# Accumulating DMAs for the cross-block spectrum sums, in-place complex sums, and a two-phase order of exponentials

## The chip, the cores and the metric

The kernel runs on one core of a Trainium2 chip. The metric is the device time in microseconds (us) of one execution; smaller is better. One execution is also recorded by the hardware profiler, and all stretches below are in microseconds from the start of that execution. A kernel's time is the median of its runs. Kernels are compared only within the same rounds.

## The reference, cut to what matters

The program blends two branches with a gate. Branch A is a state-space convolution: a kernel K of length 2048 for each of 512 channels is generated from 128 complex modes, and the input is convolved with it by a Fourier transform. Branch B routes the two highest-scoring rows through a small gated network and adds the result to them.

```python
P  = exp(dt * (A_re + 1j*A_im) * l)                  # modes x 2048 lags
K  = einsum("dn,dnl,dn->dl", C, P, dt*B).real        # kernel of the convolution
y  = irfft(rfft(pad(u)) * rfft(pad(K)))[:L] + u*Dskip
...
return g * y + (1 - g) * b       # g: sigmoid gate; b: x plus the routed rows
```

The kernel does the convolution in two blocks of 1024 rows. The output spectrum of block 1 is a sum over blocks: X1 times K0 plus X0 times K1, both complex. That sum (the "cross-block" sum) is what the change is about. Everything is done in two halves of 256 channels (half 0, half 1), and each half's spectrum in two quarters.

## The kernel before

The program lists operations with their reads, writes and a cost estimate, and a list scheduler fixes the order of instructions on each engine when the kernel is built. The hardware then follows that order. VectorE's `tensor_tensor` operations all come from one helper, `TT`, so in the profile they share one line (L399 before, L400 after).

The products of one quarter, as VectorE does them:

```python
for blk in blks:                       # block 1 first, then block 0
    TT(v4(PA), xv(blk), kv(0, 0), MUL, ...)          # 2048 columns
    if blk == 1:                       # the cross-block sum
        TT(v4(PC), xv(0), kv(1, 0), MUL, ...)
        TT(PA, PA, PC, ADD, ...)                     # 2048 columns
    TT(v4(PBb), xv(blk), kv(0, 1), MUL, ...)
    if blk == 1:
        TT(v4(PC), xv(0), kv(1, 1), MUL, ...)
        TT(PBb, PBb, PC, ADD, ...)
    TT(v1(YY, 0), v1(PA, 0), v1(PBb, 1), SUB, ...)   # complex sums, 1024 columns
    TT(v1(YY, 1), v1(PA, 1), v1(PBb, 0), ADD, ...)
    TT(sd(0), y(0), y(1), ADD, ...)                  # into X, for the inverse
    TT(sd(1), y(0), y(1), SUB, ...)
```

The inverse transform multiplies X by a constant matrix G on TensorE, block 1 before block 0. ScalarE scales half 0's result into a buffer YA, and a DMA that adds (an accumulating DMA, issued by GpSimd) puts it on the output rows:

```python
AC(YA(...), pb(...), ACTF.Copy, ..., scale=gate)
P.op(POOL, lambda g: g.dma_start(u, YA(...), accum_op=ADD), ..., cost=1.0, nbytes=262144, dma=True)
```

The front (the first part of the program, up to the end of the kernel generation) makes two tables. Table 1 and table 2 both need exponentials and sines on ScalarE; the two functions live in different activation tables. All exponentials come first, in phase 0, and then everything of phase 1:

```python
exps1(0); exps2(0)
... routing()                          # tanh, silu in phase 1
tab1(0, (1, 1)); forward(); tab2(0, (1, 1)); tab1(1, (1, 1))
```

Of the kernel before, what the change touches and what calls it, by code (L numbers as in the profile page):

```python
# [13 lines left out]
ACTF = mybir.ActivationFunctionType  # L14
ALU = mybir.AluOpType
# [39 lines left out]
class Op:  # L55
    __slots__ = ("eng", "fn", "deps", "cost", "tset", "prio", "idx", "pos", "start", "end", "sem", "n", "bl", "vc", "tag", "nbytes", "dma", "name", "alt")


class Prog:
# [4 lines left out]
    def __init__(self):  # L64
        self.bufs, self.ops, self.boost, self.bias = [], [], 0.0, {DVE: 0.4}

    def op(self, eng, fn, rd=(), wr=(), cost=0.2, tset=None, prio=0.0, tag="", n=1, nbytes=0, dma=False):
        o = Op()
        o.alt = None
        if isinstance(eng, tuple):  # L70
            o.alt = dict(zip(eng, zip(fn, cost)))
            eng, fn, cost = eng[0], fn[0], min(cost)
# [34 lines left out]
    def schedule(self):  # L107
# [25 lines left out]
        while left:  # L133
            best = None
            for e0 in ENGS:
                for o in ready[e0]:
                    if o.tset is not None and o.tset != phases[ph[0]]:
                        continue
                    e = e0
                    if o.alt is not None:  # L140
                        e = min(o.alt, key=lambda x: max(free[x], rt[o.idx]) + o.alt[x][1] + self.bias.get(x, 0.0))
                    st = max(free[e], rt[o.idx])
                    key = (st, -o.bl - o.prio)
                    if best is None or key < best[0]:
                        best = (key, o, e)
# [190 lines left out]
KB = 1024  # L336


def bass_gated_mix__ssm_conv_s4__moe_arch_mod__prompt_kernel(nc, A_u, A_A_re, A_A_im, A_B_re, A_B_im, A_C_re, A_C_im, A_log_dt, A_Dskip,
# [24 lines left out]
    with ExitStack() as es:  # L364
# [3 lines left out]
        sems = {e: es.enter_context(nc.semaphore("s_" + e)) for e in ENGS}  # L368
        dsem = [es.enter_context(nc.semaphore("d%d" % i)) for i in range(90)]
        block = es.enter_context(nc.Block())  # L370
# [49 lines left out]
        def DMA(pairs, rd, wr, nbytes, eng=SP, **k):  # L420
            return P.op(eng, lambda h: [h.dma_start(o, i) for o, i in pairs], rd, wr, cost=0.5 * len(pairs), n=len(pairs), nbytes=nbytes, dma=True, **k)

        o_ = [190 * KB]
        def small(name, nbytes, dt):
# [35 lines left out]
        KA = [B("ka0", oG, 64 * 84 * 2), B("ka1", oE, 64 * 84 * 2)]  # L460
        KC = [B("kc0", oD + 28 * KB, 3 * KB), B("kc1", oE + 11 * KB, 3 * KB)]
        KP = B("kp", oD, 2 * NKP + 1536)
        CO = [B("co%d" % i, oD + 22 * KB + 512 * i, 512) for i in range(2)]
        KK = [B("kk0", oC, 16 * KB), B("kk1", oF, 16 * KB)]
        G = B("g", oF + 16 * KB, 16 * KB)
        PA = B("pa", oI, 4 * KB); PBb = B("pb", oI + 4 * KB, 4 * KB); PC = B("pc", oI + 8 * KB, 4 * KB); YY = B("yy", oI + 12 * KB, 4 * KB); YA = B("ya", oI + 16 * KB, 4 * KB)

# [159 lines left out]
        def routing():  # L627
# [13 lines left out]
            CP(SG(0, 128, 0, (1, 16)), SGB(0, 128, 16, (1, 16)), [(SGB, "r")], [(SG, "r")])  # L641
            AC(SG(0, 128, 16, (1, 16)), SGB(0, 128, 0, (1, 16)), ACTF.Tanh, [(SGB, "s")], [(SG, "t")], scale=0.5, tset=1)
            TS(SGB(0, 128, 32, (1, 16)), SG(0, 128, 16, (1, 16)), 0.5, MUL, [(SG, "t")], [(SGB, "g")], s2=0.5, op1=ADD)
# [24 lines left out]
            STT(MSB(0, 128, 0, (1, 1)), R(35), CF(0, 128, 145, (1, 1)), R(38), MUL, ADD, [K("m1"), K("s0"), CF], [(MSB, 0)])  # L668
            AC(R(39), MSB(0, 128, 0, (1, 1)), ACTF.Tanh, [(MSB, 0)], [K("th")], scale=0.5, tset=1)
            TS(MSB(0, 128, 1, (1, 1)), R(39), 0.5, MUL, [K("th")], [(MSB, 1)], s2=0.5, op1=ADD)  # L670
# [32 lines left out]
            DMA([(WD(0, 128, 0, (D, 14), (1, D)), dr(B_w_down, 0, (D, 128), (128 * D, 14), (1, D)))], [], [WD], 1835008)  # L703
            AC(hb(2), hb(0), ACTF.Silu, [(HB, 0)], [(HB, 2)], tset=1)
            TT(hb(3), hb(2), hb(1), MUL, [(HB, 2), (HB, 1)], [(HB, 3)])
# [121 lines left out]
        def products(h, qd, blks):  # L827
# [12 lines left out]
            kk = lambda blk, part: [(KK[h], (blk, part, qd))]  # L840
            for blk in blks:
                TT(v4(PA), xv(blk), kv(0, 0), MUL, kx(blk) + kk(0, 0), [PA])
                if blk == 1:
                    TT(v4(PC), xv(0), kv(1, 0), MUL, kx(0) + kk(1, 0), [PC])
                    TT(PA(0, 128, 0, (1, 2048)), PA(0, 128, 0, (1, 2048)), PC(0, 128, 0, (1, 2048)), ADD, [PA, PC], [PA])
                TT(v4(PBb), xv(blk), kv(0, 1), MUL, kx(blk) + kk(0, 1), [PBb])
                if blk == 1:
                    TT(v4(PC), xv(0), kv(1, 1), MUL, kx(0) + kk(1, 1), [PC])
                    TT(PBb(0, 128, 0, (1, 2048)), PBb(0, 128, 0, (1, 2048)), PC(0, 128, 0, (1, 2048)), ADD, [PBb, PC], [PBb])
                TT(v1(YY, 0), v1(PA, 0), v1(PBb, 1), SUB, [PA, PBb], [(YY, 0)])  # L850
                TT(v1(YY, 1), v1(PA, 1), v1(PBb, 0), ADD, [PA, PBb], [(YY, 1)])
                y = lambda pm: YY(0, 128, pm * 512, (1024, 2), (1, 512))
                sd = lambda pm: X(0, 128, h * 8192 + blk * 4096 + pm * 1024 + 2 * qd * 256, (2048, 2), (1, 512))
                kw = lambda pm: [xk(h, blk, part, pm, ft) for part in range(2) for ft in (2 * qd, 2 * qd + 1)]
                TT(sd(0), y(0), y(1), ADD, [YY], kw(0))
                TT(sd(1), y(0), y(1), SUB, [YY], kw(1))
        ivp = [(2, 0), (2, 1), (3, 0), (3, 1)]
        ivb = [PB("iv%d" % i, a, b) for i, (a, b) in enumerate(ivp)]
        ni = [0]
        def inverse(h):  # L860
            for blk in (1, 0):
                bufs = {}
                for q in range(2):
                    for t2 in range(2):
                        for par in range(2):
# [17 lines left out]
                            if h == 0 or blk == 1:  # L883
                                for e in range(2):
                                    tb = blk * 8 + (2 * t2 + e) * 2 + par
                                    AC(YA(0, 128, t2 * 1024 + (2 * e + par) * 256, (1, HC)), pb(0, 128, e * 256, (1, HC)), ACTF.Copy, [pb.buf, (SG, "g")], [(YA, (par, t2, e))], scale=SG(0, 128, 32 + tb, (1, 1)))
                                if par == 1:
                                    tbs = [blk * 8 + 4 * t2 + k for k in range(4)]
                                    u = U(0, 128, (blk * 8 + 4 * t2) * D + h * HC, (D, 4), (1, HC))
                                    P.op(POOL, lambda g, u=u, t2=t2: g.dma_start(u, YA(0, 128, t2 * 1024, (HC, 4), (1, HC)), accum_op=ADD), [(YA, (p_, t2, e)) for p_ in range(2) for e in range(2)] + [(U, ("x", tb)) for tb in tbs], [(U, ("o", tb, h)) for tb in tbs], cost=1.0, nbytes=262144, dma=True)  # L890
                                continue
# [18 lines left out]
        exps1(0)  # L910
        exps2(0)
        DMA([(bass.AP(park.tensor, 0, [[NM * 256, 128], [1, NM * 256]]), ST(0, 128, 0, (1, NM * 256)))], [ST], [PK], 655360)
# [6 lines left out]
        P.boost = 30.0  # L919
        tab2(0, (1, 1))  # L920
        P.boost = -30.0
        tab1(1, (1, 1))
        P.boost = 0.0
# [6 lines left out]
        for h_ in range(2):  # L930
            P.op(POOL, lambda h, h_=h_: h.memset(CO[h_](0, 128, 0, (1, HC)), 0.0), [], [CO[h_]], cost=0.4)  # L931
        tab2(1, (1, 1))
        kspec(0)
# [60 lines left out]
```

## Time and profile before

| | before |
|---|---|
| median of 3 runs, us | 188.85 (187.95 to 189.13) |
| span of the profiled run, us | 187.5 |
| VectorE / TensorE / ScalarE / GpSimd busy, us | 157.1 / 139.4 / 126.5 / 12.3 |

The page of the kernel before has the busy time of each engine, and below it the span in 40 equal slices of 4.7 us: each digit is the busy share of a slice in tenths (PEclk: the granted TensorE clock).

```profile
...
PE 139.4 (74%) x1318; PEld 90.7 (48%) x1318; DVE 157.1 (84%) x232; ACT 126.5 (67%) x210; POOL 12.3 (7%) x17
...
PE   0000599675999999999994997379879999375791
...
DVE  0629124999999699999689999999989999999962
...
PEclk9999999999996999999999999958999999999998
...
```

VectorE (DVE) is idle early and full from slice 7 (counted from 0) nearly to the end. The view of chosen stretches gives numbers to that: the columns are the stretch, its length, then the busy time and instruction count of each engine, the clock, the share of the DMA engines and their rate.

```profile
...
core 0: us, PE busy (x) PEld busy (x) DVE busy (x) ACT busy (x) POOL busy (x), PEclk, DMA share, GB/s
20.70:28.40 7.70, 7.66 (x25) 3.00 (x26) 1.22 (x1) 7.69 (x15) 0.00 (x0) 1.00 1.17 262
32.00:47.00 15.00, 10.33 (x49) 4.63 (x48) 14.97 (x49) 14.11 (x23) 0.00 (x0) 1.00 0.84 296
47.00:97.00 50.00, 49.96 (x533) 27.51 (x531) 46.22 (x65) 39.74 (x69) 0.57 (x2) 0.97 0.28 85
...
139.00:179.20 40.20, 31.92 (x289) 27.78 (x289) 39.75 (x47) 17.22 (x32) 7.91 (x6) 1.00 0.40 60
...
```

VectorE is busy 1.22 of 7.7 us before the first sine, and 39.75 of 40.2 us in the last product stretch. TensorE is full in 47 to 97. Of the late stretch, the view of groups by shape tells what VectorE does (count, busy us, mean ns, idle before):

```profile
...
L399 DVE TENSOR_TENSOR AR<-AR 128x2048 bf16<-128x2048 bf16 x38 | 44.6, 1218 | 0.2
L399 DVE TENSOR_TENSOR AR<-AR 128x1024 bf16<-128x1024 bf16 x38 | 24.6, 684 | 0.3
...
```

Between 107 and 180 us it works 38 wide operations of 1.22 us with no idle time worth naming. Eight of them are the cross-block additions.

Accumulating DMAs exist already: six of 256 KB, and the view of DMAs (the queue, how many, KB each, median us) shows 4.8 us from issue to landing.

```profile
...
AR<-AR POOLq DMA_DIRECT2D x6, 256.0 KB, 4.8
...
```

### The profile page before, as it was taken

The page shows a single profiled execution, that of the slowest core. Times are in us where ns is not written, and L with a number is a line of the kernel's source. Part 1 is how long each engine was busy: PE and PEld are TensorE (multiplying, and loading weights), DVE is VectorE, ACT ScalarE, POOL GpSimd, SP SyncE. Part 2 cuts the span into 40 slices and gives each one's busy share as a digit, 9 for nine tenths or more (in the row PEclk, how much of TensorE's full clock was granted, in tenths as well). Part 3 has the DMA queues.
Part 4 walks back from the last instruction along what each step waited for, and adds up shares of the span by engine and source line. Part 5 has one row for each costly group of instructions (what it writes and reads, how often), then busy time and mean ns, then how long its engine had stood idle before and what let it go on. Part 6 is the DMA issues. An engine that isn't in the chain of part 4 may idle for free.

```text
span 187.5 us, 3219 instructions
## 1 busy us (share of the span) xinstructions
PE 139.4 (74%) x1318; PEld 90.7 (48%) x1318; DVE 157.1 (84%) x232; ACT 126.5 (67%) x210; POOL 12.3 (7%) x17
## 2 busy tenths in 40 slices
PE   0000599675999999999994997379879999375791
PEld 0000236232673444466561366278568888254680
DVE  0629124999999699999689999999989999999962
ACT  3699998999999763389999967637455573402400
POOL 8000000000000000000100000000000050500500
PEclk9999999999996999999999999958999999999998
DMA  5999999994039202200097000000840039591295
GB/s 98 309 300 357 278 258 264 405 378 108 3 91 355 61 0 56 56 3 0 19 416 310 0 3 0 2 0 3 273 180 0 0 40 151 77 154 33 33 146 157
DMA packets 33504, 25.20 MB, mean 134 GB/s; under 512 B 21449, under 2 KB 30802, under 8 KB 33106
## 3 DMA queue, kind: packets, MB, share of 16 engines
q1 hardware_dynamic: 28978, 23.10, 39.9%
q0 software_dynamic: 3168, 1.57, 7.7%
q10 hardware_dynamic: 1344, 0.33, 1.2%
q8 instruction: 10, 0.16, 0.4%
q14 instruction: 4, 0.03, 0.1%
HBM read 17.79 MB, written 2.75 MB: 110 GB/s over the span
## 4 chain that ended last, share of the span: by engine, by line
PE 45%; DVE 32%; ACT 7%; SPq 6%; DMA 4%; issue 3%; DVEq 0%
DVE AR L399 30%; PE ps L732 15%; PE ps L777 6%; PE ps L747 6%; SPq L495 6%; DMA AR<-c_fwd 4%; PE ps L875 4%; PE ps L791 3%; ACT AR L410 3%; ACT AR L414 2%; ACT AR L418 2%; PE ps L750 2%; PE ps L710 2%; PE ps L699 1%; PE ps L813 1%
## 5 line engine op out<-in xcount | busy, mean ns | idle before, releaser
L399 DVE TENSOR_TENSOR AR<-AR 128x1024 bf16<-128x1024 bf16 (+7 forms) x142 | 127.6, 949 | 11.2 <-DMA AR<-in_A_A_re_dram 6.0
L414 ACT ACTIVATE AR<-ps 128x1024 bf16<-128x1024 f32 (+4 forms) x55 | 42.2, 796 | 26.3 <-PE ps L813 11.8
L410 ACT ACTIVATE AR<-AR 128x512 bf16<-128x512 f32 (+5 forms) x73 | 50.4, 755 | 5.6 <-DVE AR L399 2.6
L732 PE MATMUL ps<-AR 128*128 128x512 bf16 x128 | 33.2, 413 | 24.4 <-DMA AR<-c_fwd 20.7
L875 PE MATMUL ps<-AR 128*128 128x256 bf16 x256 | 29.6, 273 | 7.8 <-DVE AR L399 7.8
L732 PEld LDWEIGHTS ps<-AR 128*128 128x128 bf16 x128 | 13.1, 106 | 42.1 <-DMA AR<-c_fwd 20.7
L875 PEld LDWEIGHTS ps<-AR 128*128 128x128 bf16 x256 | 24.7, 98 | 11.6 <-DVE AR L399 8.7
L410 ACT ACTIVATE AR<-ps,AR 128x256 bf16<-128x256 f32 (+1 forms) x40 | 19.8, 575 | 14.4 <-PE ps L875 13.5
L813 PE MATMUL ps<-AR 128*128 128x256 bf16 x160 | 19.2, 273 | 4.7 <-ACT AR L414 4.4
L813 PEld LDWEIGHTS ps<-AR 128*128 128x128 bf16 x160 | 15.0, 98 | 8.6 <-ACT AR L414 6.3
L414 DVE CAST AR<-ps 128x1024 bf16<-128x1024 f32 x6 | 7.3, 1218 | 13.1 <-PE ps L732 9.8
L747 PE MATMUL ps<-AR 128*128 128x512 bf16 x64 | 16.2, 389 | 0.0
L418 ACT ACTIVATE AR<-AR 128x256 int32<-128x256 f32 (+1 forms) x40 | 16.2, 468 | 0.1
L777 PE MATMUL ps<-AR 128*128 128x84 bf16 x256 | 13.7, 221 | 2.8 <-DVE AR L399 2.4
L777 PEld LDWEIGHTS ps<-AR 128*128 128x128 bf16 x256 | 12.7, 110 | 5.2 <-DVE AR L399 2.7
L890 POOL DMA_DIRECT2D AR<-AR x6 | 7.9, 1490 | 76.7 <-ACT AR L410 76.7
L403 DVE TENSOR_SCALAR AR<-AR 128x1024 int32<-128x1024 int32 (+5 forms) x22 | 11.4, 527 | 0.0
L747 PEld LDWEIGHTS ps<-AR 128*128 128x128 bf16 x64 | 5.8, 98 | 5.9 <-issue 0.2
L905 PE MATMUL ps<-AR 128*128 128x512 bf16 x16 | 6.2, 385 | 2.5 <-ACT AR L410 2.5
L791 PE MATMUL ps<-AR 128*32 128x128 bf16 (+1 forms) x96 | 6.4, 383 | 0.7 <-ACT AR L414 0.7
L931 POOL MEMSET AR<- 128x256 bf16 x2 | 0.6, 312 | 88.2 <-PE ps L777 88.2
L906 PE MATMUL ps<-AR 128*128 128x512 bf16 x16 | 6.1, 379 | 0.0
(48 smaller groups left out, 71.2 us busy)
## 6 DMA issues: line engine op xcount, KB each, us to landing
AR<-c_ksp SPq DMA_DIRECT2D x1, 2752.0 KB, 10.2
AR<-in_A_u_dram SPq DMA_DIRECT2D x2, 1024.0 KB, 7.7
AR<-c_fwd SPq DMA_DIRECT2D x1, 2048.0 KB, 8.1
AR<-c_fwdn SPq DMA_DIRECT2D x8, 256.0 KB, 3.8
AR<-c_inv SPq DMA_DIRECT2D x1, 2048.0 KB, 7.6
out_dram<-AR SPq DMA_DIRECT2D x16, 128.0 KB, 2.2
AR<-in_B_w_gate_dram SPq DMA_DIRECT2D x1, 1792.0 KB, 9.9
AR<-in_B_w_up_dram SPq DMA_DIRECT2D x2, 896.0 KB, 10.9
```

What stands on the lines that cost most here:

```text
L399: return P.op(DVE, lambda h: h.tensor_tensor(out=o, in0=a, in1=b, op=op), rd, wr, cost=tt_cost(o, a, b), **k)
L403: return P.op(DVE, lambda h: h.tensor_scalar(out=o, in0=a, scalar1=s1, scalar2=None, op0=op0), rd, wr, cost=c, **k)
L410: return P.op(ACT, lambda h: h.activation(out=o, in_=a, func=func, scale=scale, bias=bias), rd, wr, cost=0.185 + nel(o) * 0.833e-3 + (0.09 ...
L414: return P.op((ACT, DVE), (lambda h: h.activation(out=o, in_=a, func=ACTF.Copy), lambda h: h.tensor_copy(o, a)), rd, wr, cost=(0.185 + n * ...
L418: return P.op((ACT, DVE), (lambda h: h.activation(out=o, in_=a, func=ACTF.Copy, scale=c), lambda h: h.tensor_scalar(out=o, in0=a, scalar1= ...
L495: P.op(SP, lambda h: h.dma_start_transpose(PRM(0, 128, i * D, (1, D)), dr(prm[i], 0, (128, D), (1, 128))), [], [(PRM, i)], cost=1.25, nbyt ...
L732: last = h.matmul(o, F(0, 128, ((par * 4 + st) * 2 + part) * 512 + ft * 128, (1, 128)), U(0, 128, (blk * 8 + st * 2 + par) * D, (1, D)), s ...
L747: last = h.matmul(o, ng(0, 128, (st * 2 + part) * 128, (1, 128)), U(0, 128, (blk * 8 + st * 2 + 1) * D, (1, D)), start=False, stop=(st == ...
L777: last = hh.matmul(pb(0, 128, (g - b0) * 84, (1, 84)), TP[h][1 - part](0, 128, g * 128, (1, 128)), TQ[h][1 - part](0, 128, g * 84, (1, 84) ...
L791: last = hh.matmul(pb(32 * g, 32, c4, (256, njg), (4, 64)), lw, KA[h](0, 128, c4 + 4 * (base[0] + g), (16, njg), (84, 64)), start=True, st ...
L813: last = hh.matmul(pb(0, 128, n * 256, (1, 256)), KP(0, 128, u * 2048 + tau * 128, (1, 128)), KC[h](0, 128, jg * 256, (1, 256)), start=(k ...
L875: last = hh.matmul(pb(0, 128, e * 256, (1, 256)), G(0, 128, ((par * 2 + part) * 4 + ft) * 512 + (2 * t2 + e) * 128, (1, 128)), X(0, 128, h ...
```

## The change

Intent: VectorE is the limit, so take the eight cross-block additions off it and let DMAs add; form the complex sums in place; and let table 1's sines begin before table 2's exponentials, when VectorE is idle.

```diff
+        def accum(o, i, rd, wr, nbytes):
+            P.op(POOL, lambda h: h.dma_start(o, i, accum_op=ALU.add), rd, wr, cost=1.4, nbytes=nbytes, dma=True)
...
+        PAB = [(SL[0], SL[2]), (SL[4], SL[5])]
+        PCD = [[(SL[1], SL[3])] * 2, [(SL[6], SL[7]), (SL[8], SL[9])]]
...
                 TT(v4(PA), xv(blk), kv(0, 0), MUL, kx(blk) + kk(0, 0), [PA])
-                if blk == 1:
-                    TT(v4(PC), xv(0), kv(1, 0), MUL, kx(0) + kk(1, 0), [PC])
-                    TT(PA(...), PA(...), PC(...), ADD, [PA, PC], [PA])
                 TT(v4(PBb), xv(blk), kv(0, 1), MUL, kx(blk) + kk(0, 1), [PBb])
                 if blk == 1:
-                    (the same for PBb)
-                TT(v1(YY, 0), v1(PA, 0), v1(PBb, 1), SUB, [PA, PBb], [(YY, 0)])
-                TT(v1(YY, 1), v1(PA, 1), v1(PBb, 0), ADD, [PA, PBb], [(YY, 1)])
+                    for part in range(2):
+                        p, q = (PA, PBb)[part], PCD[h][qd][part]
+                        TT(v4(q), xv(0), kv(1, part), MUL, kx(0) + kk(1, part), [q])
+                        accum(p(0, 128, 0, (1, 2048)), q(0, 128, 0, (1, 2048)), [q], [p], 524288)
+                TT(v1(PA, 0), v1(PA, 0), v1(PBb, 1), SUB, [PBb], [PA])
+                TT(v1(PA, 1), v1(PA, 1), v1(PBb, 0), ADD, [PBb], [PA])
...
-        exps2(0)
+        exps2(2)
...
-        tab2(0, (1, 1))
+        tab2(0, (3, 3))
-        tab1(1, (1, 1))
+        tab1(1, (3, 3))
...
-        tab2(1, (1, 1))
+        tab2(1, (3, 3))
```

Tanh and silu move to phase 3 too (`tset=3`). Left out of the diff: the plain renaming of the output accumulates to `accum`, the sums' new operands (PA in place of YY), a scheduler setting that is renamed with its value kept, a few more semaphores, and the moving of one small buffer.

More of the change, by code (lines that the diff above doesn't have):

```diff
@@ L55 @@
 class Op:
-    __slots__ = ("eng", "fn", "deps", "cost", "tset", "prio", "idx", "pos", "start", "end", "sem", "n", "bl", "vc", "tag", "nbytes", "dma", "name", "alt")
+    __slots__ = ("eng", "fn", "deps", "cost", "tset", "prio", "idx", "pos", "start", "end", "sem", "n", "bl", "vc", "tag", "nbytes", "dma", "name", "alt", "lean")
 class Prog:
@@ L64, in __init__ @@
     def __init__(self):
-        self.bufs, self.ops, self.boost, self.bias = [], [], 0.0, {DVE: 0.4}
+        self.bufs, self.ops, self.boost, self.lean = [], [], 0.0, 0.4
     def op(self, eng, fn, rd=(), wr=(), cost=0.2, tset=None, prio=0.0, tag="", n=1, nbytes=0, dma=False):
@@ L69, in op @@
         o.alt = None
+        o.lean = self.lean
         if isinstance(eng, tuple):
@@ L140, in schedule @@
                     if o.alt is not None:
-                        e = min(o.alt, key=lambda x: max(free[x], rt[o.idx]) + o.alt[x][1] + self.bias.get(x, 0.0))
+                        e = min(o.alt, key=lambda x: max(free[x], rt[o.idx]) + o.alt[x][1] + (o.lean if x == DVE else 0.0))
                     st = max(free[e], rt[o.idx])
@@ L368, in bass_gated_mix__ssm_conv_s4__moe_arch_mod__prompt_kernel @@
         sems = {e: es.enter_context(nc.semaphore("s_" + e)) for e in ENGS}
-        dsem = [es.enter_context(nc.semaphore("d%d" % i)) for i in range(90)]
+        dsem = [es.enter_context(nc.semaphore("d%d" % i)) for i in range(120)]
         block = es.enter_context(nc.Block())
@@ L460, in bass_gated_mix__ssm_conv_s4__moe_arch_mod__prompt_kernel @@
         KA = [B("ka0", oG, 64 * 84 * 2), B("ka1", oE, 64 * 84 * 2)]
-        KC = [B("kc0", oD + 28 * KB, 3 * KB), B("kc1", oE + 11 * KB, 3 * KB)]
+        KC = [B("kc0", oD + 23 * KB, 3 * KB), B("kc1", oE + 11 * KB, 3 * KB)]
         KP = B("kp", oD, 2 * NKP + 1536)
@@ L465, in bass_gated_mix__ssm_conv_s4__moe_arch_mod__prompt_kernel @@
         G = B("g", oF + 16 * KB, 16 * KB)
-        PA = B("pa", oI, 4 * KB); PBb = B("pb", oI + 4 * KB, 4 * KB); PC = B("pc", oI + 8 * KB, 4 * KB); YY = B("yy", oI + 12 * KB, 4 * KB); YA = B("ya", oI + 16 * KB, 4 * KB)
+        SL = [B("sl%d" % i, o, 4 * KB) for i, o in enumerate([oI + 4 * KB * k for k in range(4)] + [oD + 26 * KB, oE + 16 * KB] + [oC + 4 * KB * k for k in range(4)])]
+        PAB = [(SL[0], SL[2]), (SL[4], SL[5])]
+        PCD = [[(SL[1], SL[3])] * 2, [(SL[6], SL[7]), (SL[8], SL[9])]]
+        YA = B("ya", oI + 16 * KB, 4 * KB)
         mis = [PB("mis%d" % i, 3, i) for i in range(2)]
@@ L641, in routing @@
             CP(SG(0, 128, 0, (1, 16)), SGB(0, 128, 16, (1, 16)), [(SGB, "r")], [(SG, "r")])
-            AC(SG(0, 128, 16, (1, 16)), SGB(0, 128, 0, (1, 16)), ACTF.Tanh, [(SGB, "s")], [(SG, "t")], scale=0.5, tset=1)
+            AC(SG(0, 128, 16, (1, 16)), SGB(0, 128, 0, (1, 16)), ACTF.Tanh, [(SGB, "s")], [(SG, "t")], scale=0.5, tset=3)
             TS(SGB(0, 128, 32, (1, 16)), SG(0, 128, 16, (1, 16)), 0.5, MUL, [(SG, "t")], [(SGB, "g")], s2=0.5, op1=ADD)
@@ L668, in routing @@
             STT(MSB(0, 128, 0, (1, 1)), R(35), CF(0, 128, 145, (1, 1)), R(38), MUL, ADD, [K("m1"), K("s0"), CF], [(MSB, 0)])
-            AC(R(39), MSB(0, 128, 0, (1, 1)), ACTF.Tanh, [(MSB, 0)], [K("th")], scale=0.5, tset=1)
+            AC(R(39), MSB(0, 128, 0, (1, 1)), ACTF.Tanh, [(MSB, 0)], [K("th")], scale=0.5, tset=3)
             TS(MSB(0, 128, 1, (1, 1)), R(39), 0.5, MUL, [K("th")], [(MSB, 1)], s2=0.5, op1=ADD)
@@ L703, in routing @@
             DMA([(WD(0, 128, 0, (D, 14), (1, D)), dr(B_w_down, 0, (D, 128), (128 * D, 14), (1, D)))], [], [WD], 1835008)
-            AC(hb(2), hb(0), ACTF.Silu, [(HB, 0)], [(HB, 2)], tset=1)
+            AC(hb(2), hb(0), ACTF.Silu, [(HB, 0)], [(HB, 2)], tset=3)
             TT(hb(3), hb(2), hb(1), MUL, [(HB, 2), (HB, 1)], [(HB, 3)])
@@ L841, in products @@
             for blk in blks:
+                PA, PBb = PAB[qd]
                 TT(v4(PA), xv(blk), kv(0, 0), MUL, kx(blk) + kk(0, 0), [PA])
-                if blk == 1:
-                    TT(v4(PC), xv(0), kv(1, 0), MUL, kx(0) + kk(1, 0), [PC])
-                    TT(PA(0, 128, 0, (1, 2048)), PA(0, 128, 0, (1, 2048)), PC(0, 128, 0, (1, 2048)), ADD, [PA, PC], [PA])
                 TT(v4(PBb), xv(blk), kv(0, 1), MUL, kx(blk) + kk(0, 1), [PBb])
                 if blk == 1:
-                    TT(v4(PC), xv(0), kv(1, 1), MUL, kx(0) + kk(1, 1), [PC])
-                    TT(PBb(0, 128, 0, (1, 2048)), PBb(0, 128, 0, (1, 2048)), PC(0, 128, 0, (1, 2048)), ADD, [PBb, PC], [PBb])
-                TT(v1(YY, 0), v1(PA, 0), v1(PBb, 1), SUB, [PA, PBb], [(YY, 0)])
-                TT(v1(YY, 1), v1(PA, 1), v1(PBb, 0), ADD, [PA, PBb], [(YY, 1)])
-                y = lambda pm: YY(0, 128, pm * 512, (1024, 2), (1, 512))
+                    for part in range(2):
[4 more added lines that the diff above has]
+                TT(v1(PA, 1), v1(PA, 1), v1(PBb, 0), ADD, [PBb], [PA])
+                y = lambda pm: PA(0, 128, pm * 512, (1024, 2), (1, 512))
                 sd = lambda pm: X(0, 128, h * 8192 + blk * 4096 + pm * 1024 + 2 * qd * 256, (2048, 2), (1, 512))
                 kw = lambda pm: [xk(h, blk, part, pm, ft) for part in range(2) for ft in (2 * qd, 2 * qd + 1)]
-                TT(sd(0), y(0), y(1), ADD, [YY], kw(0))
-                TT(sd(1), y(0), y(1), SUB, [YY], kw(1))
+                TT(sd(0), y(0), y(1), ADD, [PA], kw(0))
+                TT(sd(1), y(0), y(1), SUB, [PA], kw(1))
         ivp = [(2, 0), (2, 1), (3, 0), (3, 1)]
@@ L889, in inverse @@
                                     u = U(0, 128, (blk * 8 + 4 * t2) * D + h * HC, (D, 4), (1, HC))
-                                    P.op(POOL, lambda g, u=u, t2=t2: g.dma_start(u, YA(0, 128, t2 * 1024, (HC, 4), (1, HC)), accum_op=ADD), [(YA, (p_, t2, e)) for p_ in range(2) for e in range(2)] + [(U, ("x", tb)) for tb in tbs], [(U, ("o", tb, h)) for tb in tbs], cost=1.0, nbytes=262144, dma=True)
+                                    accum(u, YA(0, 128, t2 * 1024, (HC, 4), (1, HC)), [(YA, (p_, t2, e)) for p_ in range(2) for e in range(2)] + [(U, ("x", tb)) for tb in tbs], [(U, ("o", tb, h)) for tb in tbs], 262144)
                                 continue
```

## The prediction

> **What bounds it now.** Activity by stretches: VectorE is busy 14.97 of 15.0 us in 32 to 47, 46.2 of 50 in 47 to 97, 24.9 of 25.3 in 97 to 122, 39.75 of 40.2 in 139 to 179. From 32 us to 179 us it is the limit, and TensorE beside it in 47 to 97 (49.96 of 50). Before 32 us it is nearly idle (1.22 of 7.7 us in 20.7 to 28.4), because ScalarE runs 41 exponentials back to back (21.5 us, 614 ns each in the groups, one per 0.52 us in the timeline) before the first sine at 29.7 us. After 139 us the chain of waits is VectorE's tensor_tensor nearly alone until the last inverse transform (176 us) and the 8 us tail. In 122 to 179 VectorE does 30 operations of 128x2048 (1217 ns each) and 34 of 128x1024 (685 ns): the spectrum products.
>
> **What the change does.**
>
> 1. Removes 8 of those 2048-wide additions: 8 x 1.15 us (start to start) = 9.2 us of VectorE. In-place sums change no count.
> 2. Adds 8 accumulating DMAs of 512 KB on the GpSimd queue. The six accumulates of today (256 KB, 512 B runs) take 4.8 us from issue to landing, at about 140 GB/s with all 16 DMA engines full, so about 1.9 us is data and 3 us fixed. My estimate for 512 KB in 4 KB runs is 6 to 7 us alone, with 3 to 3.7 us of all 16 engines, and 1.3 to 1.7 us of GpSimd. The Trainium skill ("DMA: Bandwidth & Descriptors", SWDGE vs HWDGE vs iDMA) says that only GpSimd can issue an accumulate; the trace agrees, all six sit there. So all 14 accumulates go through one queue in order.
> 3. Lets the first table's sines start when 32 exponentials are done, about 23.7 us, plus a table load. The trace shows a load as 1.28 us, as the skill says ("ScalarE: Activation LUTs", What ACT_TABLE_LOAD costs); the change adds two, 2.6 us, on an engine that has slack after 57 us.
>
> **Critical path.** Front: VectorE starts table 1's products some 5 us earlier in its idle time, evacuations become more timely (TensorE is idle 4.7 us in 32 to 47), and the second exponentials fall while the engines are occupied with table 1. Both VectorE and TensorE then reach the end of the first kernel generation (97 us) about 4 us earlier (2 to 6).
>
> Products: 9.2 us less work, but new waits. In half 0 both quarters share the scratch, so the second quarter's third product waits for the first accumulate: after its two free products VectorE stalls some 3 us, then about 1.5 more for the second; the load of the inverse matrix (2 MB, 7.6 us) falls there too. In half 1 the scratch is separate and the stall is 1 to 3 us. Net 4 us gained (0 to 8).
>
> 188.85 - 4 - 4 = about 180.5 us. 80% range 175 to 187. Faster by over 2%: 0.80; within 2%: 0.16; slower: 0.04.
>
> **What would show it.** First sine at about 25 us instead of 29.7; four table loads; VectorE over 60% busy in 24 to 32; last kernel-generation matmul of half 0 near 88 to 89 instead of 92.5; VectorE 128x2048 operations in the products down to 22; accumulates landing in 6 to 7 us; VectorE idle of 3 to 7 us in the products, released by DMA, mostly in half 0; tail of 8 us unchanged.
>
> **What would make it wrong.** Accumulates much slower than estimated (512 KB over 8 us, or the queue blocked behind one that waits): most of the 9 us is given back, about 185. Large runs that go at plain copy speed: stalls vanish, about 176. ScalarE, with two more table loads, delaying table 2's sines: the front gains nothing.

## More of the kernel before

How the kernel ends is seen in TensorE's timeline (start, length, engine, line, operation; in brackets the idle time before it and who ended it):

```profile
...
163.85 3.67 PE L875 MATMUL ps<-AR 128*128 128x256 bf16 x32 [3.25 <-DVE AR L399]
171.04 1.92 PE L875 MATMUL ps<-AR 128*128 128x256 bf16 x16 [3.53 <-DVE AR L399]
...
175.97 5.41 PE L875 MATMUL ps<-AR 128*128 128x256 bf16 x48 [1.04 <-DVE AR L399]
...
181.33 1.91 PE L875 MATMUL ps<-AR 128*128 128x256 bf16 x16
...
```

L875 is the inverse of half 1. Its block 1 is fed in two portions as VectorE finishes them, at 163.85 and at 171.04; block 0 follows at 175.97. After the last block-1 sums the kernel has 187.5 - 171.04 = 16.5 us to go.

## The result

| | before | after |
|---|---|---|
| median, us | 188.99 (4 runs) | 200.07 (198.79 to 201.37, 4 runs) |
| ratio, 95% interval | | 1.061 (1.051 to 1.070) |
| span of the profiled run, us | 187.5 | 198.2 |
| VectorE busy, us | 157.1 | 150.0 |
| VectorE waiting for accumulates, us | 0 | 14.2 |

A ratio here is always the mean time of one kernel's runs over the mean of the other's runs of the same rounds, so it is not quite the ratio of the medians quoted. Executions over 1.5% slower than the fastest of the same kernel are left out of the means. Medians are of all runs. The result is correct. The kernel is 6% slower.

The page of the kernel after:

```profile
...
PE 144.5 (73%) x1318; PEld 92.8 (47%) x1318; DVE 150.0 (76%) x229; ACT 127.9 (65%) x207; POOL 19.3 (10%) x25
...
PE   0000699718999999999957983978999864647990
...
DVE  0629069997899989996699999947539997749451
...
PEclk9999999966987999999999999799999979785899
...
```

VectorE has lost 7 us of work and has gained holes: 4, 7, 5 and 3 in slices 26 to 29 (counted from 0), and 7, 7 and 4 in slices 33 to 35. The groups by shape of the late stretch answer to those of before:

```profile
...
L400 DVE TENSOR_TENSOR AR<-AR 128x2048 bf16<-128x2048 bf16 x30 | 35.0, 1218 | 3.9 <-DMA AR<-AR 3.9
L400 DVE TENSOR_TENSOR AR<-AR 128x1024 bf16<-128x1024 bf16 x38 | 24.4, 686 | 10.6 <-DMA AR<-AR 10.3
...
```

Exactly eight wide operations are gone, 44.6 - 35.0 = 9.6 us. In their place VectorE idles 3.9 + 10.6 us before these operations, nearly all of it ended by a DMA (3.9 + 10.3). The view of waits has the totals (us, times, longest):

```profile
...
DVE AR L400 <- DMA AR<-AR: 14.2, 5, 5.0
ACT AR L411 <- DMA AR<-AR: 14.1, 2, 13.4
...
```

VectorE's timeline has the five waits one by one, three in half 0 and two in half 1:

```profile
...
131.03 1.22 DVE L400 TENSOR_TENSOR AR<-AR 128x2048 bf16<-128x2048 bf16 x1 [1.36 <-DMA AR<-AR]
134.81 6.88 DVE L400 TENSOR_TENSOR AR<-AR 128x2048 bf16<-128x2048 bf16 x8 [2.56 <-DMA AR<-AR]
146.71 1.89 DVE L400 TENSOR_TENSOR AR<-AR 128x1024 bf16<-128x1024 bf16 x3 [5.01 <-DMA AR<-AR]
...
166.66 5.74 DVE L400 TENSOR_TENSOR AR<-AR 128x1024 bf16<-128x1024 bf16 x7 [1.32 <-DMA AR<-AR]
...
176.37 9.23 DVE L400 TENSOR_TENSOR AR<-AR 128x1024 bf16<-128x1024 bf16 x13 [3.96 <-DMA AR<-AR]
...
```

The first two come before wide products: they are the second quarter's, which wait for the shared scratch. The other three come before the complex sums, which wait for their operands. ScalarE waits too, once for 13.4 us. What they wait for is on the GpSimd queue (timeline; a product accumulate takes 0.86 to 1.02 us of it; the brackets as above):

```profile
...
126.00 2.00 POOL L425 DMA_DIRECT2D AR<-AR  x2 [31.52 <-DVE AR L400]
132.55 0.86 POOL L425 DMA_DIRECT2D AR<-AR  x1 [4.55 <-DVE AR L400]
136.33 0.86 POOL L425 DMA_DIRECT2D AR<-AR  x1 [2.93 <-DVE AR L400]
158.75 0.86 POOL L425 DMA_DIRECT2D AR<-AR  x1 [21.56 <-DVE AR L400]
159.89 3.49 POOL L425 DMA_DIRECT2D AR<-AR  x3 [0.28 <-DVE AR L400]
164.50 0.88 POOL L425 DMA_DIRECT2D AR<-AR  x1 [1.12 <-DVE AR L400]
165.63 0.86 POOL L425 DMA_DIRECT2D AR<-AR  x1 [0.26 <-DVE AR L400]
...
```

The first four, at 126.0 to 136.3, are half 0's product accumulates; 158.75, 159.89, 164.50 and 165.63 begin half 1's. The group of three at 159.89 is one product accumulate and two output accumulates behind it. Asked for each of them, the trace shows these times from issue to landing: 5.0 us for the first, which starts with the DMA engines to itself; 7.6 for the second; 11.7 and 10.3 for the third and fourth, which share the engines with the 2 MB load of the inverse matrix; then 4.7, 6.7, 8.6 and 10.7 in half 1. The median of all of the eight is 8.1:

```profile
...
AR<-AR POOLq DMA_DIRECT2D x8, 512.0 KB, 8.1
...
```

And the end of the kernel, TensorE's timeline again:

```profile
...
179.52 3.60 PE L882 MATMUL ps<-AR 128*128 128x256 bf16 x16 [3.96 <-DVE AR L400]
...
183.12 2.60 PE L882 MATMUL ps<-AR 128*128 128x256 bf16 x16
...
185.67 5.40 PE L882 MATMUL ps<-AR 128*128 128x256 bf16 x48
...
191.02 1.91 PE L882 MATMUL ps<-AR 128*128 128x256 bf16 x16
...
```

The last block-1 sums of half 1 now come at 179.52, where before they came at 171.04. From there TensorE works without a pause to 193.0 us. Of the 10.7 us by which the span grew, 179.52 - 171.04 = 8.5 us had come by then, and 18.7 - 16.5 = 2.2 us came after it. TensorE's last stretch is 1.2 us of that (13.5 us against 12.3): its first two groups of 16 matmuls take 3.60 + 2.60 us, where they took 1.92 + 1.91 us before, 2.4 us more (the granted clock is 0.50 through the first group and part of the second), and the pause of 1.04 us before block 0 is gone. The other 1.0 us comes after the last matmul (5.2 us against 4.2). The Trainium skill ("TensorE: Matmul & The Clock Gate", What's actually happening) says that TensorE drops to half clock after an idle window of about 3.4 us, that the window runs freely, and that about as long of work brings the clock back. The half clock after a wait of 3.96 us agrees. The length of a wait alone doesn't decide, though: in the kernel before, the wait of 3.53 us at 171.04 left the clock full, and in this kernel a shorter one, of 2.46 us before 160.25, was followed by half clock (0.50 from 161.25 to 163.5, and 16 matmuls in 3.26 us).

In front, ScalarE's timeline shows the two phases as intended:

```profile
...
24.10 1.28 ACT L243 ACT_TABLE_LOAD   x1
25.40 2.00 ACT L411 ACTIVATE AR<-AR 128x1024 bf16<-128x1024 int16 x2
...
40.77 1.28 ACT L411 ACT_TABLE_LOAD   x1
...
47.78 1.28 ACT L243 ACT_TABLE_LOAD   x1
...
```

Sines start at 25.40 us (before: 29.71), and there are two more table loads of 1.28 us. Still, the last matmul group of half 0's kernel generation starts at 93.39 us, against 92.04 before (it ends at 92.52, which is the prediction's 92.5). TensorE's timelines, before and after:

```profile
...
92.04 0.48 PE L777 MATMUL ps<-AR 128*128 128x84 bf16 x8
...
93.39 0.47 PE L784 MATMUL ps<-AR 128*128 128x84 bf16 x8
...
```

### The profile page after: what moved, and what is told of

The parts are those of the page before. It is cut to its first block, busy times and chain, and to the rows that moved or that the text cites. A ratio compares the mean times of both kernels' runs of the same rounds, so it can differ in the third digit from the quotient of the medians.

```text
span 198.2 us, 3218 instructions
## 1 busy us (share of the span) xinstructions
PE 144.5 (73%) x1318; PEld 92.8 (47%) x1318; DVE 150.0 (76%) x229; ACT 127.9 (65%) x207; POOL 19.3 (10%) x25
## 3 DMA queue, kind: packets, MB, share of 16 engines
q1 hardware_dynamic: 28978, 23.10, 38.5%
## 4 chain that ended last, share of the span: by engine, by line
PE 36%; DVE 34%; DMA 19%; SPq 6%; issue 2%; POOL 1%; DVEq 0%
DVE AR L400 27%; DMA AR<-AR 14%; PE ps L739 12%; PE ps L882 7%; SPq L502 6%; PE ps L754 5%; DMA AR<-c_fwd 4%; PE ps L784 2%; DVE AR L404 2%; DVE AR L415 2%; PE ps L717 2%; PE ps L798 2%; PE ps L757 2%; PE ps L706 1%; POOL AR L425 1%
## 5 line engine op out<-in xcount | busy, mean ns | idle before, releaser
L400 DVE TENSOR_TENSOR AR<-AR 128x1024 bf16<-128x1024 bf16 (+8 forms) x134 | 118.4, 933 | 25.1 <-DMA AR<-AR 14.2
L415 ACT ACTIVATE AR<-ps 128x1024 bf16<-128x1024 f32 (+4 forms) x52 | 41.0, 823 | 24.7 <-PE ps L820 12.5
L411 ACT ACTIVATE AR<-AR 128x512 bf16<-128x512 f32 (+4 forms) x73 | 50.7, 756 | 5.7 <-DVE AR L400 3.2
L739 PE MATMUL ps<-AR 128*128 128x512 bf16 x128 | 32.9, 409 | 22.1 <-DMA AR<-c_fwd 21.4
L882 PE MATMUL ps<-AR 128*128 128x256 bf16 x256 | 35.6, 302 | 10.9 <-DVE AR L400 10.1
L411 ACT ACTIVATE AR<-ps,AR 128x256 bf16<-128x256 f32 (+1 forms) x40 | 20.1, 562 | 25.5 <-DMA AR<-AR 14.1
L882 PEld LDWEIGHTS ps<-AR 128*128 128x128 bf16 x256 | 27.3, 108 | 17.7 <-DVE AR L400 11.2
L739 PEld LDWEIGHTS ps<-AR 128*128 128x128 bf16 x128 | 12.9, 105 | 39.4 <-DMA AR<-c_fwd 21.4
L820 PE MATMUL ps<-AR 128*128 128x256 bf16 x160 | 20.0, 277 | 4.8 <-ACT AR L415 4.8
L425 POOL DMA_DIRECT2D AR<-AR x14 | 14.9, 1207 | 79.3 <-DVE AR L400 62.2
L820 PEld LDWEIGHTS ps<-AR 128*128 128x128 bf16 x160 | 15.1, 99 | 9.3 <-ACT AR L415 7.2
L754 PE MATMUL ps<-AR 128*128 128x512 bf16 x64 | 16.9, 400 | 0.0
L415 DVE CAST AR<-ps 128x1024 bf16<-128x1024 f32 (+2 forms) x9 | 8.8, 982 | 10.1 <-PE ps L739 7.4
L784 PE MATMUL ps<-AR 128*128 128x84 bf16 x256 | 12.8, 210 | 1.7 <-ACT AR L415 1.1
L784 PEld LDWEIGHTS ps<-AR 128*128 128x128 bf16 x256 | 11.8, 103 | 4.0 <-ACT AR L415 1.8
L404 DVE TENSOR_SCALAR AR<-AR 128x1024 int32<-128x1024 int32 (+5 forms) x22 | 11.5, 528 | 0.6 <-ACT AR L411 0.5
L754 PEld LDWEIGHTS ps<-AR 128*128 128x128 bf16 x64 | 5.9, 100 | 6.7 <-issue 1.0
L912 PE MATMUL ps<-AR 128*128 128x512 bf16 x16 | 6.1, 383 | 3.1 <-ACT AR L411 2.8
L407 DVE SCALAR_TENSOR_TENSOR AR<-ps,AR 128x256 bf16<-128x256 f32 x8 | 3.5, 480 | 4.9 <-PE ps L882 4.6
L419 DVE TENSOR_SCALAR AR<-AR 128x256 int32<-128x256 f32 (+1 forms) x24 | 6.2, 300 | 1.2 <-ACT AR L411 1.2
```

The lines of the kernel that those rows point to most:

```text
L400: return P.op(DVE, lambda h: h.tensor_tensor(out=o, in0=a, in1=b, op=op), rd, wr, cost=tt_cost(o, a, b), **k)
L404: return P.op(DVE, lambda h: h.tensor_scalar(out=o, in0=a, scalar1=s1, scalar2=None, op0=op0), rd, wr, cost=c, **k)
L411: return P.op(ACT, lambda h: h.activation(out=o, in_=a, func=func, scale=scale, bias=bias), rd, wr, cost=0.185 + nel(o) * 0.833e-3 + (0.09 ...
L415: return P.op((ACT, DVE), (lambda h: h.activation(out=o, in_=a, func=ACTF.Copy), lambda h: h.tensor_copy(o, a)), rd, wr, cost=(0.185 + n * ...
L419: return P.op((ACT, DVE), (lambda h: h.activation(out=o, in_=a, func=ACTF.Copy, scale=c), lambda h: h.tensor_scalar(out=o, in0=a, scalar1= ...
L425: P.op(POOL, lambda h: h.dma_start(o, i, accum_op=ALU.add), rd, wr, cost=1.4, nbytes=nbytes, dma=True)
```

## The experiments

Four theories stood after the result. T: the bytes of the accumulates are the loss, since they arrive later than VectorE needs them. F: the phase split in front is. I: the in-place sums serialise the products. O: the static order of the instructions is bad, and the bytes don't matter. Each expectation below names the theory or rival that it tests; those that came later (R, L, C, H, N and A) are stated there. Unless it is said otherwise, runs have three rounds.

### Parts alone (e1, e2, e3)

e1 puts only the phase split into the kernel before:

```diff
-        exps2(0)
+        exps2(2)
-        tab2(0, (1, 1)) ...
+        tab2(0, (3, 3)) ...      # and tab1(1), tab2(1); tanh, silu tset=3
```

> The kernel before with only the two-phase exponentials (table 2's behind table 1's angles, tanh and silu in the last phase). Theory T (accumulates are the loss; the front is bounded by the forward matmuls): 188 to 191 us, four table loads, last kernel-generation matmul of half 0 within 1.5 us of the 92.5 us of before. Rival F (the phase split is the loss): 195 us or more. The step of the prediction under test (front gains 4 us): 184 to 186 us.

Measured: 191.56 us, ratio 1.013 (1.005 to 1.021). The split alone does not gain; it loses a little (by 0.5% to 2.1%).

e2 is the change with that part undone.

> The change without its phase split (all exponentials first, as before): accumulating DMAs and in-place sums only. T: 197 to 201 us, VectorE waits of 10 us or more on accumulates. F: 191 us or less.

Measured: 196.79 us, ratio 1.040 (1.033 to 1.047), with 14.3 us of VectorE's waits on accumulates. The time is just under the range of T. F falls: most of the loss is here. The two parts nearly add: 1.3% and 4.0% against 6.1%.

e3 is e2 with the additions given back to VectorE:

```diff
-                        accum(p(...), q(...), [q], [p], 524288)
+                        TT(p(...), p(...), q(...), ADD, [p, q], [p])
```

> As e2, but each cross-block product is added by VectorE (tensor_tensor, as before) instead of by a DMA: in-place sums and the new scratch buffers alone. T: 187 to 191 us, like before. Rival I (sums in place serialise the products): 195 us or more.

Measured: 189.93 us, ratio 1.006 (0.997 to 1.015). In-place sums and new buffers cost at most 1.5% and perhaps nothing; I falls.

### The bytes taken away (e4, e13)

e4 leaves every instruction of the change in its place, on every engine, and only narrows what the DMA moves:

```diff
-                        accum(p(0, 128, 0, (1, 2048)), q(0, 128, 0, (1, 2048)), [q], [p], 524288)
+                        accum(p(0, 128, 0, (1, 64)), q(0, 128, 0, (1, 64)), [q], [p], 524288)
```

This no longer computes the reference: most of the cross-block sum is missing. (The comparison with the reference passed all the same, as its tolerance doesn't see so small a part. It is not a usable kernel.)

> The change with every instruction in its place, but each of the 8 accumulating DMAs moves 64 of the 2048 columns (16 KB instead of 512 KB); wrong result on purpose. T (the bytes of the accumulates): 183 to 188 us, VectorE waits for accumulates under 3 us in all, ScalarE's wait of 13.4 us for an accumulate gone, tail after VectorE's last product back near 8 us. Rival O (the order of instructions or the fixed latency of a GpSimd DMA is the loss): 196 us or more.

Measured: 188.00 us, ratio 0.994 (0.987 to 1.000). Twelve us less than the change, with the same order of instructions: T is shown, and O falls as the main cause. The waits of e4:

```profile
...
ACT AR L411 <- DMA AR<-AR: 3.7, 1, 3.7
...
DVE AR L400 <- DMA AR<-AR: 2.7, 1, 2.7
...
```

VectorE's wait fell from 14.2 to 2.7 us, and ScalarE's from 14.1 to 3.7. The 2.7 us that are left are one accumulate of 16 KB that landed only after 8.1 us: it was issued at 133.32, at the same time as the 2 MB load. The tail did not come back to 8 us, as I had expected: VectorE's last product ends near 174.9 us and the span at 186.7. TensorE sets the end here: from the last block-1 sums of half 1, at 168.8, it works 12.8 us without a pause, and the span ends 17.9 us after them. It is at half clock at first here too (16 matmuls in 3.44 us), after a wait of 2.81 us that is not for an accumulate.

e13 does the same to e2, that is without the phase split.

> e2 (no phase split) with each accumulate cut to 64 of 2048 columns, every instruction in its place; wrong result on purpose. If the bytes are the loss also without the split: 183 to 187 us against 196.8 of e2, i.e. 10 us or more less; and if the split costs something of its own, 1 to 4 us less than e4 (188.0). If the rest of e2's loss were order: 193 us or more.

Measured: 183.46 us (180.97 to 186.16), ratio 0.962 (0.941 to 0.982); two of the four runs were slow, the fast ones are 183.21 and 180.97. With the bytes gone, e2's loss of 4% turns into a gain of 4%. VectorE's waits for accumulates are nearly gone:

```profile
...
DVE AR L400 <- DMA AR<-AR: 0.3, 1, 0.3
...
```

So VectorE's 9.6 us were worth having, and the accumulates' bytes cost 13 us by the medians of e2 and e13. It also shows the split once more: e4 is slower than e13 by 4.5 us by the medians and by 5.9 by the fast runs.

### Which queueing (e5, e6, e7, e8)

e5 keeps the order, but the load of the inverse matrix waits for half 0's four accumulates: `g_op.deps |= {o.idx for o in accs[0]}`, set after the scheduling.

> The change with every instruction in its place, but the queue of the inverse-matrix load (2 MB) waits until half 0's four accumulates have landed. Theory C (part of the loss is that this load and the accumulates share the 16 DMA engines): the third and fourth accumulate land in 5 to 8 us instead of 11.7 and 10.3, VectorE's waits for accumulates fall from 14.2 to 8 to 10 us, total 196 to 199 us, the inverse starting later (146 to 150 us instead of 142) takes some of it back. Rival (no contention, the accumulates are slow by themselves): landings stay over 10 us and the total 200 us.

Measured: 200.42 us, ratio 1.055 (1.051 to 1.060). The contention is real: the third and fourth accumulate landed in 4.6 and 6.0 us instead of 11.7 and 10.3. VectorE's waits fell only from 14.2 to 11.5 us, and the time missed the expected 196 to 199 us: half 0's waits went from 8.9 to 4.4, but half 1's last wait from 4.0 to 7.1, as its two accumulates now stood behind two output accumulates on the GpSimd queue (a group of four at 164.10). So nothing was gained. The load, too, now came later, and the inverse waited for it, as TensorE's timeline shows:

```profile
...
150.68 1.89 PE L884 MATMUL ps<-AR 128*128 128x256 bf16 x8 [7.40 <-DMA AR<-c_inv]
...
```

Two transfers want the 16 DMA engines in the same 10 us, and whichever goes second is late. The Trainium skill ("DMA: Bandwidth & Descriptors", Issuing engines are not separate DMA queues) says that DMAs of all issuing engines run on the same 16 engines and interleave; this pair of runs agrees, with 11.7 against 4.6 us for one and the same transfer.

e6 keeps the order except on GpSimd, where half 0's first two output accumulates go ahead of half 1's product accumulates.

> The change with every instruction in its place except on the GpSimd queue, where half 0's first two output accumulates (256 KB) stand ahead of half 1's product accumulates. Theory H (head-of-line blocking: ScalarE waits 13.4 us because the output accumulates stand behind product accumulates whose operands VectorE has not made yet): ScalarE's wait falls below 6 us, the first output store starts before 162 us instead of 168.5, total 196 to 199.5 us. Rival (only VectorE's waits matter): ScalarE's wait falls too, but the total stays within 0.5 us of 200.

Measured: 197.38 us, ratio 1.038 (1.035 to 1.041); e5, e7 and e8 on the same chip had 1.051 to 1.058. ScalarE's wait for accumulates is gone (it no longer appears among its waits), VectorE's fell from 14.2 to 12.1 us, and the first output store starts at 160.4 us instead of 168.5. So some 2.5 to 4 us of the loss are the queue's order (2.7 by the medians of the change and e6, 2.3 to 3.9 against e8, e5 and e7): output accumulates that were ready at 155 us stood behind product accumulates whose operands VectorE had not made. One queue takes everything in turn.

e7 gives the second quarter of half 0 scratch of its own in two dead buffers.

```diff
-        PCD = [[(SL[1], SL[3])] * 2, ...
+        SX = [B("sx0", OHR.off, 4 * KB), B("sx1", AL.off, 4 * KB)]
+        PCD = [[(SL[1], SL[3]), (SX[0], SX[1])], ...
```

> The change with separate scratch for the second quarter of half 0 (two dead 4 KB buffers), so that its products need not wait for the first quarter's accumulates. Scheduled anew. If the shared scratch is a main loss, as the prediction had it: VectorE's waits for accumulates fall by 4 us or more and the total is 195 to 197 us. Theory T (the bytes through the DMA engines limit): the waits move to the sums that need the accumulates, total 198 to 200 us.

Measured: 201.26 us, ratio 1.058 (1.055 to 1.062). VectorE's waits are 15.3 us, no less than before. The two waits at the shared scratch are gone, but those before half 0's sums are now 3.44 + 6.27 = 9.7 us, where half 0 had 8.9 in all. The shared scratch, which the prediction named, only chose where VectorE waits.

e8 tells the scheduler what accumulates cost here:

```diff
-                dma_free[e] = t0 + o.nbytes / self.DMA_BW
+                dma_free[e] = t0 + o.nbytes / (150.0e3 if e == POOL else self.DMA_BW)
                 # and 1.6 us of latency, and POOL and SP share the DMA engines
```

> The change as written, but its list scheduler is told what the trace shows of accumulates: 150 GB/s instead of 300, 1.6 us of latency instead of 1.2, and one set of DMA engines for the GpSimd and Sync queues. Theory T (raw cost of the accumulates, that no order hides): 193 to 198 us, still slower than before. Rival O (only the order was bad): 186 us or less.

Measured: 199.72 us, ratio 1.051 (1.047 to 1.055). VectorE's waits fell to 9.3 us, but the time stayed above the 193 to 198 us that T had expected. With eight accumulates, knowing their cost hardly helps this scheduler.

### Fewer accumulates (e9 to e12)

With the corrected scheduler and without the phase split, only some of the eight additions go to DMAs:

```diff
-                        accum(...)
+                        if (h, qd, part) in ACCS: accum(...)
+                        else: TT(p(...), p(...), q(...), ADD, [p, q], [p])
```

> Accumulating DMAs for both sums of both quarters of half 0 only (four of the eight), VectorE adds in half 1; exponentials in one phase as before; in-place sums; the scheduler told the measured cost of accumulates, as in e8. Theory N (what counts is how many accumulates are in flight when VectorE needs their sums, together with the inverse-matrix load): 193 to 196 us, waits of VectorE for accumulates 6 us or more, tail back near 8 us. Rival A (each accumulate costs about the same, so four cost half of what eight cost in e2): 193 us here, in e10 and in e11 alike.

> The same with the four accumulates in half 1 only. N: 191 to 195 us; VectorE waits only at the end, and the last inverse starts late, tail of 11 us or more. A: 193 us.

> The same with four accumulates, one in each quarter of each half: the first sum of a quarter by DMA, the second by VectorE, which thereby has work while the DMA runs. N: 183 to 187 us, faster than before, waits of VectorE for accumulates under 2 us. A: 193 us.

> The best of the 256 choices by the corrected scheduler: five accumulates (one, two, one, one by quarter; half 0's second quarter has two) and separate scratch for half 0's second quarter. N: 182 to 187 us, within 1.5 us of e11. A: 194 us.

| | accumulates | us | ratio (95%) | VectorE's waits for them, us |
|---|---|---|---|---|
| e3 | none | 189.93 | 1.006 (0.997 to 1.015) | 0 |
| e9 | 4, all in half 0 | 191.62 | 1.008 (1.001 to 1.016) | 1.8 |
| e10 | 4, all in half 1 | 192.01 | 1.009 (1.001 to 1.018) | 3.4 |
| e11 | 4, one in each quarter | 188.22 | 0.988 (0.981 to 0.995) | 0 |
| e12 | 5, one or two in each quarter | 186.96 | 0.983 (0.977 to 0.990) | 2.1 |
| e2 | 8 | 196.79 | 1.040 (1.033 to 1.047) | 14.3 |

Four accumulates cost nothing like half of what eight cost, and four are worth 2% more when they are spread, one to a quarter, so that VectorE adds the other sum while the DMA runs. Theory N had the order right and the sizes wrong: e9 came 1.4 us under its range and e11 1.2 us over, so that 3.4 us lie between them where N expected 6 or more. The waits are only part of that difference: in e9 VectorE also waits 4.17 us for TensorE at 139.86. In e11 a product accumulate lands in 4.6 to 5.2 us, as one does that has the engines to itself, and VectorE doesn't wait for one:

```profile
...
AR<-AR POOLq DMA_DIRECT2D x4, 512.0 KB, 5.1
...
```

e12 beats both kernels, by 1.7% over before. Its end shows the half clock too: 16 matmuls of half 1's inverse take 3.42 us after a wait of 3.35 us. One control is missing: no run has the corrected scheduler and no accumulate, so how much of the gain of e11 and e12 over before is the scheduler's is not shown. That spreading matters is, since e9, e10 and e11 share the scheduler.

### The front (e14 to e18)

e14 asks whether the two added table loads make e1 slower. The nine exponentials of the second phase become scaled copies, so that no table changes; all else keeps its place. Its output is wrong, which doesn't matter for the time.

> e1 (phase split alone) with the second phase's nine exponentials replaced by scaled copies, so that the two added table loads vanish and every instruction else keeps its place; wrong result on purpose. Theory R (the split loses because routing's transposes on TensorE wait behind VectorE's table 1 products, which now come first, and the forward matmuls queue behind them): within 1 us of e1, 190.5 to 192 us, gather matmuls still at about 50 us. Rival L (the two table loads, 2.6 us on ScalarE): 187 to 189.5 us, gather at 48 us.

Measured: 191.42 us, ratio 1.012 (1.001 to 1.022), the same as e1; its trace has two table loads, as before. The table loads are not the cause.

e15 puts the split into e12.

> e12 (five accumulates, the best so far) with the phase split put back. If the split gains nothing also where accumulates are few: 187.5 to 190 us, 1 to 3 us more than e12. If it only failed because of the queue at the end: 185 us or less.

Measured: 190.48 us, ratio 1.005 (0.997 to 1.014), that is 3.5 us more than e12 (expected were 1 to 3). The split loses also where accumulates are few.

The remaining idea was the routing chain. Its four transposes sit on TensorE's in-order queue among the forward matmuls, and each waits for small VectorE steps. In e1, VectorE does table 1's products between those steps, and TensorE stands still for it longer. TensorE's timeline of e1:

```profile
...
40.91 0.33 PE L655 MATMUL ps<-AR 128*128 128x128 f32 x1 [2.25 <-DVE AR L403]
44.33 0.47 PE L655 MATMUL ps<-AR 128*128 128x128 f32 x1 [3.09 <-DVE AR L403]
45.47 3.17 PE L732 MATMUL ps<-AR 128*128 128x512 bf16 x8 [0.66 <-DVE AR L414]
...
50.30 1.75 PE L677 MATMUL ps<-AR 128*128 128x2 bf16 x64
...
```

And of the kernel before:

```profile
...
44.16 1.90 PE L732 MATMUL ps<-AR 128*128 128x512 bf16 x8 [3.13 <-ACT AR L414]
...
47.82 1.76 PE L677 MATMUL ps<-AR 128*128 128x2 bf16 x64
...
```

The two routing waits sum to 2.25 + 3.09 = 5.3 us (1.0 us before), and the gather matmuls (L677) start at 50.30 us against 47.82. But before, TensorE waits 3.13 us for ScalarE in the same place. So only 1.3 us of the 2.5 is a later start of these forward matmuls (45.47 against 44.16), and 1.3 us is half clock: eight of them take 3.17 us instead of 1.90. The gather alone decides little: in e13, without the split, the clock halved there after the same wait for ScalarE (3.14 us), the gather came at 51.20, and e13 is the fastest of all. e16, e17 and e18 add one rule to the scheduler: a routing step may go first on VectorE if it is ready within 1.5 us.

```diff
-                    key = (st, -o.bl - o.prio)
+                    key = (st - (1.5 if e == DVE and 100.0 <= o.prio < 200.0 else 0.0), -o.bl - o.prio)
```

> e1 (phase split alone) with one rule added to the scheduler: a VectorE step of the routing chain may go first if it is ready within 1.5 us, even if table work could start at once. Theory R (the split loses because routing steps stand behind table 1's products on VectorE and the in-order matmul queue behind routing): gather matmuls before 47 us instead of 50, 187 to 189.5 us against 191.6 of e1. Rival (the loss is elsewhere in front): 191 us or more.

> The kernel before with the same rule for routing and nothing else: control for e16 and e18. If routing bounds the front also without the split: 184 to 187 us. If not: 188 us or more.

> e12 (five accumulates, no phase split, no table change) with the same rule for routing: the version meant to beat both kernels. If the two gains add: 181 to 185 us, 2.5% or more under before. If not: 186 to 188 us, as e12.

This edit does more than its name says: the scheduler takes an operation's start from the same key (`st = best[0][0]`), so it enters each favoured step 1.5 us earlier than it can run and builds the rest of the order on times that are wrong. All three missed widely: 201.75 us (1.056), 201.07 (1.057) and 199.24 (1.048, five rounds). The gather did move, to 40.0 us in e16 and 38.5 in e17, and yet half 0's kernel generation ended 8 to 10 us later (its last matmuls start at 102.0 and 101.1 us). In e17 the other engines starve meanwhile:

```profile
...
32.00:47.00 15.00, 9.73 (x114) 6.22 (x116) 12.86 (x39) 7.59 (x12) 0.00 (x0) 0.66 0.69 261
...
```

ScalarE is busy 7.59 of these 15 us where it was busy 14.11 before, and TensorE 9.73 against 10.33, at a granted clock of 0.66 against 1.00. With the wrong times in the scheduler, these three runs do not test theory R: whether putting routing first helps stays open. That the split costs 2 to 6 us is shown by four pairs (e1 against before, the change against e2, e4 against e13, e15 against e12); that the table loads are not why is shown by e14; what in the new order is at fault stays open. One candidate of the right size is untested: in all four pairs, and in e14, the split makes VectorE 1.9 to 2.1 us busier (e1 159.0 us, before 157.1), as the scheduler, which may place some copies on ScalarE or VectorE, divided them otherwise.

## Why the prediction was wrong

The prediction said 180.5 us, in a range of 175 to 187; 200.07 was measured.

1. **What bounds the kernel, and what VectorE would shed: right.** Eight wide additions left, 9.6 us measured against 9.2. e13 shows that they are worth 4% if nothing is waited for.
2. **A single accumulate: right to a small error.** I estimated 6 to 7 us alone; it was 5.0. GpSimd spent 0.86 to 1.02 us on one, not 1.3 to 1.7.
3. **The step that failed: "Net 4 us gained (0 to 8)" in the products.** The new waits were put at 4.5 us in half 0 and 1 to 3 us in half 1, because each accumulate was costed alone. Measured are 1.36 + 2.56 + 5.01 = 8.9 us in half 0 and 1.32 + 3.96 = 5.3 us in half 1. The sum is 14.2 us of waits (3 to 7 were predicted) for 9.6 us of work, and the products' part of the change alone (e2) is 7.2 us slower by the medians, not 4 faster. What the prediction lacks in half 0 is the wait of the sums themselves, 5.01 us for an accumulate that landed in 10.3 us; in half 1 the last one landed in 10.7. Three of the four pairs of accumulates are issued 1.1 us apart, and each is fed through the same DMA engines as the one before, the load of the inverse matrix and the output accumulates. The prediction mentions the load, but adds nothing for it. That the bytes do it is shown by e4 and e13, and the load's part by e5.
4. **The stall at the shared scratch in half 0: right in size, wrong as the cost.** It was 1.36 + 2.56 = 3.9 us against 4.5. But e7 removed it and gained nothing: the waits moved to the sums.
5. **Two terms that were missing.** First, the sums that wait for the accumulates are block 1's, and the inverse begins with block 1: so the last wait delays TensorE's last 13.5 us, not only VectorE. (TensorE comes out of it at half clock, but in e4 and e11 it does so too, where no accumulate is waited for there.) "Tail of 8 us unchanged" was wrong: from VectorE's last product to the end it is 187.5 - 179.2 = 8.3 us before and 198.2 - 185.6 = 12.6 us after. The longer tail is mostly not the waits' doing: it is 10.0 us in e3, which has no product accumulates, and 11.8 in e4. There VectorE ends sooner, but TensorE's inverse sets the end, so not all of the 9.6 us could be won. Second, the GpSimd queue is one queue: I wrote that all 14 accumulates go through it in order, and listed a queue that is blocked among what could go wrong, but left its cost out. It was some 2.5 to 4 us (e6).
6. **"Both VectorE and TensorE then reach the end of the first kernel generation about 4 us earlier": wrong.** It came 1.4 us later in these two profiles. That is within the scatter of profiles: the group that starts at 92.04 before starts at 90.8 to 93.5 in the profiles of e2, e3, e12 and e13, which have no split either, and at 93.1 to 94.5 in those with it. But none with it is early, and the split costs 2 to 6 us in all pairs. The sines came early as predicted (25.40 us), and VectorE was busy 3.60 of 3.6 us from 28.4 to 32, but VectorE's early work was not what TensorE waited for: TensorE's unbroken stretch began at 45.4 us instead of 44.2. My step from "VectorE is early" to "both are early" had no measurement under it.
7. **What the case "wrong" said:** slow accumulates would give "about 185". Even the warning was too mild, since it returned only the 9 us and did not let the waits pass on to the inverse.

## What to carry to other kernels

Work handed from an engine to DMAs has to be costed as a stream, not as one transfer: list all transfers that want the DMA engines and the issuing queue in that stretch, and ask who consumes the last of them. Give a DMA only every second sum, so that the engine has its own sum to do while the DMA runs: that, with the scheduler told what accumulates cost, turned a loss of 4% into a gain of 1 to 2%. And when a chain is made to start earlier, find the wait in the trace that it releases before counting the time as won.

## What the Trainium skill lacked or had wrong

- "DMA: Bandwidth & Descriptors" gives no rate for an accumulating DMA from on-chip memory to on-chip memory. Here one of 512 KB in 4 KB runs, issued by GpSimd, lands in 4.5 to 5.2 us alone, one of 256 KB in 512 B runs in 4.2 us, and two of 512 KB issued 1.1 us apart in 5.0 and 7.6 us. The page says that GpSimd's queue is the one for accumulates; all 14 sit there.
- The same page gives no time for a small transfer beside a large one: 16 KB that is issued together with a 2 MB load landed in 8.1 us, and in 2.0 to 2.2 us in the half-0 transfers without it and the first two of half 1 (e4).
- "TensorE: Matmul & The Clock Gate" gives the idle window that costs the clock as about 3.4 us and adds that it runs freely. How uncertain this makes a single wait is shown here: 3.53 us (before) left the clock full, 3.35 us (e12) and 3.96 us (after) halved it, and so did waits well under the window, of 2.46 us (after, at 160.25) and 2.79 us (e11, at 168.82). One and the same wait in front, 3.13 to 3.14 us, left it full in before, e2 and e12 and halved it in e13.
- "ScalarE: Activation LUTs", What ACT_TABLE_LOAD costs: it counts 2.66 us for a table switch, 1.28 of load and 1.38 of drain. Here the load takes 1.28 us as it says, but the load began 0.02 us after the last exponential ended (24.08), and the next function starts 1.30 us after the load began (24.10 to 25.40), so no drain was paid beyond it.
